# K and V chunks as two interleaved half transfers, and part of one w4 piece in 8-partition transfers

## The chip, the core and the metric

The kernel runs on one core of one Trainium2 chip. The metric is the device time in microseconds (us) of one execution; the median of three executions of the kernel before is 216.05 us (215.88 to 216.5). The core has five instruction streams: TensorE (PE) for matrix products, VectorE (DVE), ScalarE (ACT), GpSimd (POOL) and SyncE (SP). Here SP computes nothing: it issues the transfers from the chip's main memory (HBM) to the on-chip memory (SBUF, 128 partitions), which 16 DMA engines carry out.

## What is computed

One decode step of a transformer block for a batch of four, one token each, width 576. The output is x + attention + MLP, all in bfloat16:

```
xn = layernorm(x)
q  = xn @ wq                          # 32 heads of 128
k, v = the last 2048 positions of the caches, 16 KV heads, each shared by 2 query heads
o  = softmax(q k^T / sqrt(128)) v
A  = o @ wo
h  = gelu(layernorm(xn) @ w1);  x1 = xn + shift(h) @ w2
B  = x1 + gelu(layernorm(x1) @ w3) @ w4     # w3: 576 x 4608, w4: 4608 x 576
out = x + A + B
```

Nearly all of the work is reading: 4 x 16 heads x 2048 positions x 128 values of K and as much of V are 64 blocks of 0.5 MB each, 67 MB together, and the weights are another 21 MB.

## The kernel before

**Chunks.** K and V are each read in 16 chunks (`NC`) of 2 MB. A chunk is one batch row and four KV heads (`NU = 4`). SBUF partition p of a chunk holds head p mod 4 and 64 successive positions, so each partition receives one run of 16 KB from HBM. A ring of four slots (`ring_t`, `NPOS = 4`) holds the chunks. `kv_pairs` (line 226) makes the list of (destination, source) pairs of one chunk; in the kernel before it has one pair, all 128 partitions.

**Transfers.** `add_dma` (line 171) issues one transfer for each pair (line 177) and lets each of them add 16 to one semaphore. SP issues in a fixed order: wq, w2, w1, w3, sixteen K chunks, sixteen V chunks with the first half of wo after the fourth of them, the second half of wo, and then w4 in five pieces. A K chunk waits until the transposes of the chunk four before it are done, a V chunk until its slot is free (lines 232 to 235). SP executes in order, so whatever stands behind a waiting transfer waits too.

**w4.** `W4_ROWS = (18, 9, 6, 2, 1)` cuts the 4608 rows of w4 into pieces of 18, 9, 6, 2 and 1 rows on each of 128 partitions (a row is 576 values, 1152 bytes). The piece numbered 1, the second, is 9 rows: 10,368 bytes on each partition. Each piece has its own semaphore, `("w4", n)`. The first piece waits for early matmuls, the others for nothing; so all five are issued one after another as soon as SP comes to them.

**Compute.** For each K chunk, PE transposes 64 blocks (line 339), DVE and ACT copy them out, and PE multiplies them with the queries (line 353). The softmax follows once for all, and then, for each V chunk, 64 small matmuls (line 420). The attention output is multiplied with wo and the MLP's hidden layer with w4, all adding into the same PSUM tile (line 437); the loop at line 547 takes the w4 pieces in the order in which they were issued, each after a wait for its transfer. The last piece, one row, is followed by two copies (lines 559 and 560) and two small transfers of the output.

**Loops.** The K and V loops on PE are hardware loops. In them a wait for a chunk is a "take": it waits until the semaphore has reached a number and takes that number off again. It is 16 in the kernel before, one transfer's worth. The four ring slots have separate semaphores.

Of the kernel before, what the change touches and what calls it, by code (L numbers as in the profile page):

```python
# [13 lines left out]
NPOS = 4  # L14
ACT_EVAC = (1, 4, 7)
WO_AT = (3.5, 15.5)
IDLE = ((3, -2.7), (7, 0.5), (5, 20.5))
HOPS = (("K", 15), ("V", 2))
W4_ROWS = (18, 9, 6, 2, 1)


# [14 lines left out]
def bass_parallel_sum__sliding_block_cached__mixer_s_mlp__decode_kernel(  # L36
# [3 lines left out]
    _, Hkv, Sk, Dh = A_k_cache.shape  # L40
    Hq = A_wq.shape[1] // Dh
    F = B_w3.shape[1]
    W = min(4096, max(256, Sk // 4))
    assert (B, D, Hkv, Dh, Hq, W, Hq // Hkv, F) == (4, 576, 16, 128, 32, 2048, 2, 4608)
    NU = 4
    NC = B * Hkv // NU
    NI = 128 // NU
    NT = W // NI
    UE = NT * Dh
# [10 lines left out]
    with ExitStack() as ctx:  # L60
        def sb(name, shape, dt):
            return ctx.enter_context(nc.sbuf_tensor(name, shape, dt))
# [4 lines left out]
        ring_t = sb("ring", [128, NPOS * UE], BF16)  # L67
# [89 lines left out]
        def add(engine, emit, waits=(), sig=None, key=0.0, inc=(), loop=None, cond=None):  # L157
            seqc[0] += 1
            prog[engine].append(Op(emit, waits, sig, key, seqc[0], inc, loop, cond))

        def tok(nm):
            if nm not in S:
                S[nm] = sem("t_" + "_".join(str(k) for k in (nm if isinstance(nm, tuple) else (nm,))))
            return nm

        def take(nm, n=1):
            return ("take", tok(nm), n)
# [3 lines left out]
        def add_dma(pairs, skey, waits=(), key=0.0, engine="sp"):  # L171
            tok(skey)
            dma_count[skey] = dma_count.get(skey, 0) + 16 * len(pairs)

            def emit(e):
                for o_, i_ in pairs:
                    e.dma_start(o_, i_).then_inc(S[skey], 16)  # L177
            add(engine, emit, waits, None, key)
            return ("dma", skey, dma_count[skey])
# [11 lines left out]
        def pool_ident(t, tag, pattern, view, key):  # L191
# [19 lines left out]
            waits=["ident_f"], sig="mU", key=-8)  # L211
# [13 lines left out]

        def kv_pairs(cache, c):
            b, gq = CH[c]
            return [(ring_t[:, (c % NPOS) * UE:(c % NPOS + 1) * UE],
                     cache[b, NU * gq:NU * gq + NU, Sk - W:Sk, :].rearrange("g (i t) d -> i g (t d)", t=NT))]

        t_done = lambda c: f"T{NBLK * c + NBLK - 1}"
        for c in range(NC):
            add_dma(kv_pairs(A_k_cache, c), ("k", c % NPOS), [t_done(c - NPOS)] if c >= NPOS else [], c)
# [4 lines left out]
        w4tile, w4cols, ev_w4, W4N = [], [], [], []  # L238
        base = 0
        for n, rc in enumerate(W4_ROWS):  # L240
            v = w4_t[:, len(w4tile) * D:(len(w4tile) + rc) * D]
            ev_w4.append(add_dma([(v, B_w4[base:base + 128 * rc, :].rearrange("(p r) n -> p (r n)", r=rc))], ("w4", n),
                                 ["hT1", "hs1"] if n == 0 else [], KT + 5 + n))
            W4N.append((len(w4tile), len(w4tile) + rc))
            for r in range(rc):
                w4tile.append(v[:, r * D:(r + 1) * D])
                w4cols.append((base + r, base + 128 * rc, rc))
            base += 128 * rc
# [68 lines left out]
        for b in range(B):  # L317
            add("dve", lambda e, b=b: e.tensor_copy(out=qp_out[:, b], in_=qp_in[:, b]), waits=["qTp", "qpad_zero"],
                sig="qT" if b == B - 1 else None, key=-29.4)
# [13 lines left out]
        def pe_T(n):  # L333
            c, k = n // NBLK, n % NBLK

            def f(e):
                ins = None
                for t in range(8):
                    ins = e.transpose(tb[n % 4][:, t, :], slot_t(c)[:, 8 * k + t, :], perm_bf[:])  # L339
                return ins  # L340
            return f

        def evac(n):
            if n % 8 in ACT_EVAC:
                return "act", lambda e: e.activation(out=ktbuf[:, n % 16], in_=tb[n % 4], func=ACTF.Copy)  # L345
            return "dve", lambda e: e.tensor_copy(out=ktbuf[:, n % 16], in_=tb[n % 4])  # L346

        def pe_SC(c):
            def f(e):
                ins = None  # L350
                for q in range(4):
                    for u in range(NU):
                        ins = e.matmul(Sps[32 * u:32 * u + 32, q, :].rearrange("p (t i) -> p t i", t=16),  # L353
                                       lhsT=Qs[:, c % NPOS, 32 * u:32 * u + 32], rhs=ktgrp[:, 4 * (c % 2) + q, :, u, :],
                                       start=False, stop=True, tile_position=(0, 32 * u), skip_group_check=True)
                return ins
            return f
# [3 lines left out]
        for c in range(NC):  # L361
            lp = ("K", c // NPOS)
            for k in range(NBLK):
                w = [take(("k", c % NPOS), 16)] if k == 0 else []
                prev = (k + 4) % 8
                w.append(evtok(prev))
                add("pe", pe_T(NBLK * c + k), waits=w, sig=f"T{NBLK * c + k}", key=NBLK * c + k, loop=lp)
                eng, f = evac(NBLK * c + k)
                add(eng, f, waits=[f"T{NBLK * c + k}"] + ([f"SC{c - 2}"] if c >= 2 else []), inc=[("evA" if eng == "act" else "evD", 1)],
                    key=NBLK * c + k + 0.2)  # L370
            add("pe", pe_SC(c - 1), waits=[take("qs")], sig=f"SC{c - 1}", key=NBLK * c + SC_AFTER + 0.5, loop=lp)
            b, gq = CH[c]
            cc = 4 * b + gq
            P(lambda e, c=c, cc=cc: e.tensor_copy(out=Qs[:, c % NPOS, :], in_=Qpad_t[:, 128 * cc:128 * cc + 128]),  # L374
              waits=["qT", "qs_zero"] + ([f"SC{c - NPOS}"] if c >= NPOS - 1 else []), inc=[("qs", 1)], key=c)
# [6 lines left out]
            waits=["rmax"], sig="negb", key=KS + 0.05)  # L382
        for q in range(4):
            add("act", lambda e, q=q: e.activation(out=P_sb[:, q, :], in_=Sps[:, q, :], func=ACTF.Exp,
                                                   bias=negb[:, 0:1], scale=scale, accum_out=rs4[:, q:q + 1]),
                waits=["negb"], sig=f"exp{q}", key=KS + 0.1 + 0.01 * q)

        for q in range(4):
# [3 lines left out]
                waits=[f"PTx{q}", "permT_bf"] + (["PT0"] if q == 3 else []), sig=f"PTy{q}", key=k0)  # L392
            add("act", lambda e, q=q: e.activation(out=PT_t[:, 512 * q:512 * (q + 1)], in_=ps[:, 4 + q % 3, :], func=ACTF.Copy),
                waits=[f"PTy{q}"], sig=f"PT{q}", key=k0 + 0.16)
# [3 lines left out]
            waits=["rinv", "ident_f"], sig="diag", key=KS + 0.82)  # L398
        add("pe", lambda e: e.matmul(rinvps, lhsT=ones_f[:], rhs=diag[:], start=True, stop=True), waits=["diag", "ones_f", "exp3"],
            sig="rinvp", key=KS + 0.9)  # L400
        add("dve", lambda e: e.tensor_copy(out=rinvB[:].rearrange("p (c u e) -> p c u e", u=NU, e=2),
                                           in_=rinvps.rearrange("p (u c e) -> p c u e", u=NU, e=2)),
            waits=["rinvp"], sig="rinvB", key=KS + 1.5)
# [9 lines left out]
        def pe_PV(c):  # L413
            b, gq = CH[c]
            o_ = OTps[:, 8 * b:8 * b + 8]

            def f(e):
                ins = None
                for t in range(NT):
                    ins = e.matmul(o_, lhsT=slot_t(c)[:, t, :], rhs=PTpad[:, c % 2, t].rearrange("p u e -> p (u e)"),  # L420
                                   start=(t == 0), stop=(t == NT - 1))
                return ins
            return f
        for c in range(NC):
            w = [f"PV{c - 2}"] if c >= 2 else [f"PT{q}" for q in range(4)] + ["mU_bf1"]
            b, gq = CH[c]
            add("dve", dve_pad(c), waits=w, inc=[(tok("pad"), 1)], key=KV + 2 * max(c - 1, 0) + 0.2)
            add("pe", pe_PV(c), waits=[take("pad"), take(("v", c % NPOS), 16)] + ([take("otn")] if b == 0 else []), sig=f"PV{c}",
                key=KV + 2 * c, loop=("V", gq))
            if b == B - 1:  # L430
                hv = lambda t, gq=gq: t[:, 0:128].rearrange("p (b h) -> p b h", b=B)[:, :, 8 * gq:8 * gq + 8]
                add("dve", lambda e, hv=hv: e.tensor_tensor(out=hv(OTn), in0=OTps.rearrange("p (b h) -> p b h", b=B), in1=hv(rinvB), op=ALU.mult),  # L432
                    waits=["rinvB", f"PV{c}"], sig=f"OTn{gq}" if gq == 3 else None, inc=[(tok("otn"), 1)] if gq < 3 else [], key=KV + 2 * c + 0.1)
# [13 lines left out]
        def pe_AO(half):  # L447
# [10 lines left out]
            waits=["OTy"], sig="ORp", key=KT - 2.5)  # L458
# [30 lines left out]
        for h in range(2):  # L489
# [3 lines left out]
                waits=[f"hs{h}", "ln1"], sig="x1" if h else "x1a", key=-29 + 0.6 * h)  # L493
# [4 lines left out]
        for h in range(2):  # L498
            add("act", lambda e, h=h: e.activation(out=h_sb[:, HALF * h:HALF * (h + 1)], in_=HTps[h], func=ACTF.Gelu_apprx_tanh),
                waits=[f"hT{h}", "x1nT"], sig="gelu_h" if h else None, key=-20 + 0.1 * h)  # L500

        segs = []
        for g in range(4):
            for k in range(3):
                first = 9 * g + 3 * k
                t = first
                while t < first + 3:
                    n = next(m for m, (a, z) in enumerate(W4N) if a <= t < z)
                    cnt = min(first + 3, W4N[n][1]) - t
                    segs.append((g, k, t - first, cnt, w4cols[W4N[n][0]][0], W4_ROWS[n], t - W4N[n][0], t == first))  # L510
                    t += cnt
# [18 lines left out]
        for k in range(3):  # L530
            add("act", lambda e, k=k: e.activation(out=h2g[:, 384 * k:384 * (k + 1)], in_=H2ps[k], func=ACTF.Gelu_apprx_tanh), waits=["h2_3"],
                sig="gelu2" if k == 2 else None, key=-0.9 + 0.1 * k)

        def pe_h2T(e):
# [7 lines left out]
            waits=["h2T"], inc=[("evA", 1)], key=-0.3)  # L542
        add("dve", lambda e: e.tensor_copy(out=h2o[:, :, 8, :], in_=H2Tb.rearrange("p (g y) -> p g y", g=4)[..., 0:B]),  # L543
            waits=["h2T"], inc=[("evD", 1)], key=-0.3)
# [51 lines left out]
        def emit_program(eng_name, engine):  # L596
# [6 lines left out]
            while i < len(ops):  # L603
# [12 lines left out]
                with engine.bass.Fori(0, len(passes), engines=OrderedEngineSet([engine.engine]), head_slot={engine.engine: 0}):  # L616
                    inner = nc.cur_bb
                    for k, op in enumerate(passes[0]):
                        emit_op(eng_name, engine, op, waited)
                        if (name, k) in HOPS:  # L620
                            engine.br_eq(hop, 0, on_true=f"hop_{name}", on_false=f"fall_{name}")
# [53 lines left out]
```

## Time and profile before

| | before |
|---|---|
| median of three executions | 216.05 us |
| the profiled execution, its own time | 216.5 us |
| its span, first to last instruction | 214.7 us |
| bytes moved | 88.65 MB |
| PE busy | 147.2 us (69%) |
| DVE busy | 76.2 us (35%) |
| ACT busy | 60.2 us (28%) |
| K transfers, 2048 KB each | 16 |
| V transfers, 2048 KB each | 16 |
| w4 transfers, 2592 / 1296 / 864 / 288 / 144 KB | 1 each |

The profile shows one execution. Its page cuts the span in 40 equal slices of 5.4 us and gives for each the busy share of every engine, of the DMA engines, and the rate of transfer. It lists the queues of the DMA engines (q1 is SP's, "instruction" queues load program code), the chain of work that ended last, and the groups of instructions. "SPq" is SP issuing a transfer. The records behind the page also hold the start, length and size of each packet that a DMA engine moved, and the times at which transfers added to their semaphores; they do not say which of the 16 engines a packet was on.

### The profile page before, as it was taken

The numbers are of one execution on the slowest core, as the hardware profiler recorded it, in microseconds if no ns is written. First come the engines' busy times: TensorE is split into PE (matmuls) and PEld (weight loads), VectorE is DVE, ScalarE is ACT, GpSimd is POOL, SyncE is SP. The second block draws the span as 40 slices with busy tenths as digits, with TensorE's granted clock in tenths as the row PEclk, the third lists the DMA queues.
The fourth block names the chain that finished last, engine by engine and source line by source line (L and its number), as shares of the span: only waits on it lengthen the run. The fifth ranks groups of instructions, "written<-read, shape, count | busy, mean of one in ns | idle before, by whom it ended". The sixth has DMA issues, their size and how long they took to land. (4 is left out here: it accounts for less than half of the span.)

```text
span 214.7 us, 5874 instructions
## 1 busy us (share of the span) xinstructions
PE 147.2 (69%) x2642; PEld 111.2 (52%) x2646; DVE 76.2 (35%) x150; ACT 60.2 (28%) x75; POOL 10.9 (5%) x37
## 2 busy tenths in 40 slices
PE   0158699799999999999997177334444333337984
PEld 0023333777888887788885047234434333335542
DVE  4303700276667767667775751110010010001000
ACT  2001210455666666566666540000000000000000
POOL 8301000000000000000000000000000000000000
PEclk9999889699999999999999755555555555555999
DMA  7999999999999999999999999999999999999992
GB/s 276 409 381 443 436 413 433 437 424 411 412 424 430 433 433 424 427 429 433 421 430 424 427 436 419 427 427 430 424 427 424 430 430 427 427 432 432 417 413 78
DMA packets 6946, 88.65 MB, mean 413 GB/s; under 512 B 780, under 2 KB 1176, under 8 KB 1944
## 3 DMA queue, kind: packets, MB, share of 16 engines
q1 hardware_dynamic: 6920, 88.50, 97.4%
q8 instruction: 8, 0.13, 0.2%
q10 hardware_dynamic: 16, 0.01, 0.0%
q14 instruction: 2, 0.02, 0.0%
HBM read 88.49 MB, written 0.00 MB: 412 GB/s over the span
## 5 line engine op out<-in xcount | busy, mean ns | idle before, releaser
L339 PEld LDWEIGHTS ps<-perm_bf,ring 128*128 128x128 bf16 x1024 | 58.8, 99 | 7.1 <-issue 6.8
L339 PE MATMUL ps<-perm_bf,ring 128*128 128x128 bf16 x1024 | 61.9, 221 | 0.0
L346 DVE COPY kt<-ps 128x1024 bf16<-128x1024 bf16 x80 | 52.3, 688 | 24.2 <-PE ps L339 23.1
L420 PE MATMUL ps<-PTpad,ring 128*128 128x8 bf16 x1024 | 29.7, 168 | 39.9 <-PEq L583 35.9
L345 ACT ACTIVATE kt<-ps 128x1024 bf16<-128x1024 bf16 x48 | 47.7, 1023 | 29.3 <-PE ps L339 29.3
L420 PEld LDWEIGHTS ps<-PTpad,ring 128*128 128x128 bf16 x1024 | 28.7, 104 | 41.1 <-issue 41.0
L560 ACT ACTIVATE out_sb<-ps 4x288 bf16<-4x288 f32 x1 | 0.4, 401 | 86.4 <-PE ps L437 86.4
L353 PE MATMUL ps<-kt,Qs 128*32 128x512 bf16 x272 | 17.8, 382 | 1.4 <-PEq L583 1.4
L409 DVE TENSOR_TENSOR PTpad<-PT,mU_bf 128x512 bf16<-128x512 bf16 x16 | 6.4, 421 | 28.2 <-PE ps L420 28.2
L432 DVE TENSOR_TENSOR OTn<-ps,rinvB 128x32 bf16<-128x32 f32 x4 | 0.8, 192 | 34.5 <-PE ps L420 34.5
L522 PE MATMUL ps<-w,x1nT 128*32 128x384 bf16 (+1 forms) x65 | 11.1, 766 | 0.4 <-DVE x1nT L497 0.4
L353 PEld LDWEIGHTS ps<-kt,Qs 128*32 128x32 bf16 x272 | 5.8, 95 | 6.8 <-issue 1.5
L374 POOL COPY Qs<-Qpad 128x128 bf16<-128x128 bf16 x16 | 4.6, 293 | 89.1 <-PE ps L353 75.9
L300 PE MATMUL ps<-kt,xnT 128*32 128x512 bf16 x32 | 3.6, 631 | 4.6 <-DMA kt<-in_A_wq_dram 4.6
L522 PEld LDWEIGHTS ps<-w,x1nT 128*32 128x32 bf16 x65 | 3.6, 115 | 5.4 <-issue 5.0
L277 PE MATMUL ps<-ident_bf,xn_bf 4*128 4x4 bf16 x8 | 0.6, 170 | 8.0 <-DVE ragsrc L270 8.0
L437 PE MATMUL ps<-w,h2T_sb 128*4 128x288 bf16 x72 | 5.1, 286 | 1.4 <-DMA w<-in_B_w_dram 1.4
L559 DVE CAST out_sb<-ps 4x288 bf16<-4x288 f32 x1 | 0.4, 446 | 14.9 <-PE ps L437 14.9
L437 PE MATMUL ps<-w,ORT 128*4 128x288 bf16 x64 | 5.0, 324 | 0.4 <-DVE ORT L459 0.4
L391 PE MATMUL ps<-kt,permT_bf 128*128 128x512 bf16 x3 | 1.8, 608 | 4.9 <-DVE kt L390 4.8
L437 PEld LDWEIGHTS ps<-w,h2T_sb 128*4 128x4 bf16 x72 | 2.8, 84 | 4.0 <-DMA w<-in_B_w_dram 3.0
L543 DVE COPY h2T_sb<-ps 128x16 bf16<-128x16 bf16 x1 | 0.2, 166 | 13.3 <-PE ps L537 13.3
(99 smaller groups left out, 65.2 us busy)
## 6 DMA issues: line engine op xcount, KB each, us to landing
ring<-in_A_k_cache_dram SPq DMA_DIRECT2D x16, 2048.0 KB, 11.5
ring<-in_A_v_cache_dram SPq DMA_DIRECT2D x16, 2048.0 KB, 16.6
w<-in_B_w_dram SPq DMA_DIRECT2D x2, 2304.0 KB, 23.0
w<-in_A_wo_dram SPq DMA_DIRECT2D x2, 2304.0 KB, 20.3
kt<-in_A_wq_dram SPq DMA_DIRECT2D x1, 4096.0 KB, 12.5
w<-in_B_w_dram SPq DMA_DIRECT2D x1, 2592.0 KB, 28.0
w<-in_B_w_dram SPq DMA_DIRECT2D x3, 576.0 KB, 14.3
w<-in_B_w_dram SPq DMA_DIRECT2D x1, 1296.0 KB, 30.7
```

Source lines behind the costliest of these rows:

```text
L300: ins = e.matmul(Qps[k][32 * g:32 * g + 32, :], lhsT=x_, rhs=w, start=(r == 0), stop=(r == 4), tile_position=(0, 32 * g), skip_group_check ...
L339: ins = e.transpose(tb[n % 4][:, t, :], slot_t(c)[:, 8 * k + t, :], perm_bf[:])
L345: return "act", lambda e: e.activation(out=ktbuf[:, n % 16], in_=tb[n % 4], func=ACTF.Copy)
L346: return "dve", lambda e: e.tensor_copy(out=ktbuf[:, n % 16], in_=tb[n % 4])
L353: ins = e.matmul(Sps[32 * u:32 * u + 32, q, :].rearrange("p (t i) -> p t i", t=16), lhsT=Qs[:, c % NPOS, 32 * u:32 * u + 32], rhs=ktgrp[:, ...
L374: P(lambda e, c=c, cc=cc: e.tensor_copy(out=Qs[:, c % NPOS, :], in_=Qpad_t[:, 128 * cc:128 * cc + 128]), waits=["qT", "qs_zero"] + ([f"SC{ ...
L391: add("pe", lambda e, q=q: e.matmul(ps[:, 4 + q % 3, :], lhsT=permT_bf[:], rhs=PTx[:, q, :], start=True, stop=True), waits=[f"PTx{q}", "pe ...
L409: return lambda e: e.tensor_tensor(out=PTpad[:, c % 2], in0=PTv[:, :, cc, :].unsqueeze(2).to_broadcast([128, NT, NU, 2]), in1=mU_bf[:].uns ...
L420: ins = e.matmul(o_, lhsT=slot_t(c)[:, t, :], rhs=PTpad[:, c % 2, t].rearrange("p u e -> p (u e)"), start=(t == 0), stop=(t == NT - 1))
L432: add("dve", lambda e, hv=hv: e.tensor_tensor(out=hv(OTn), in0=OTps.rearrange("p (b h) -> p b h", b=B), in1=hv(rinvB), op=ALU.mult), waits ...
L437: return e.matmul(ACC[h], lhsT=lhsT, rhs=rhs, start=start, stop=stop, tile_position=(0, 32 * h), skip_group_check=True)
L522: ins = e.matmul(H2ps[k][32 * g:32 * g + 32, 128 * off:128 * (off + cnt)].rearrange("p (c x) -> p c x", c=cnt), lhsT=x_, rhs=w.rearrange(" ...
```

## The change

There are two edits. First, `kv_pairs` gives two pairs for each chunk: the even partitions (`a = 0`, heads 0 and 2 of the four) and the odd ones (`a = 1`, heads 1 and 3), 64 partitions and 1 MB each. The takes of the two loops become 32. The bytes, the size of a run on one partition (16 KB) and the order of the chunks stay.

Second, `LOW8 = 1` names the w4 piece 1. Its partitions 0, 4, 8, ..., then 1, 5, 9, ..., then 2, 6, 10, ... are loaded by three transfers of 32 partitions, and the last quarter, partitions 3, 7, 11, ..., by four transfers of 8 partitions. The description of the change says that only DMA engines 0 to 7 carry those last four. The other pieces stay.

```
+LOW8 = 1
 W4_ROWS = (18, 9, 6, 2, 1)
...
         def kv_pairs(cache, c):
             b, gq = CH[c]
-            return [(ring_t[:, (c % NPOS) * UE:(c % NPOS + 1) * UE],
-                     cache[b, NU * gq:NU * gq + NU, Sk - W:Sk, :].rearrange("g (i t) d -> i g (t d)", t=NT))]
+            dst = lambda a: ring_t[a:128:2, (c % NPOS) * UE:(c % NPOS + 1) * UE]
+            src = cache[b, NU * gq:NU * gq + NU, Sk - W:Sk, :].rearrange("g (i t) d -> i g (t d)", t=NT)
+            return [(dst(a), src[:, a:NU:2, :]) for a in range(2)]
...
             v = w4_t[:, len(w4tile) * D:(len(w4tile) + rc) * D]
-            ev_w4.append(add_dma([(v, B_w4[base:base + 128 * rc, :].rearrange("(p r) n -> p (r n)", r=rc))], ("w4", n),
+            w4_src = B_w4[base:base + 128 * rc, :].rearrange("(p r) n -> p (r n)", r=rc)
+            rows = [slice(0, 128)] if n != LOW8 else [slice(a, 128, 4) for a in range(3)] + [slice(3 + a, 32 + a, 4) for a in range(0, 128, 32)]
+            ev_w4.append(add_dma([(v[a], w4_src[a]) for a in rows], ("w4", n),
                                  ["hT1", "hs1"] if n == 0 else [], KT + 5 + n))
...
-                w = [take(("k", c % NPOS), 16)] if k == 0 else []
+                w = [take(("k", c % NPOS), 32)] if k == 0 else []
...
-            add("pe", pe_PV(c), waits=[take("pad"), take(("v", c % NPOS), 16)] + ([take("otn")] if b == 0 else []), sig=f"PV{c}",
+            add("pe", pe_PV(c), waits=[take("pad"), take(("v", c % NPOS), 32)] + ([take("otn")] if b == 0 else []), sig=f"PV{c}",
```

## The prediction

> **What bounds the kernel now.** I read the DMA rows of the page first, then the chain that ended last, then SP's queue.
>
> ```profile
> span 214.7 us, 5874 instructions
> PE   0158699799999999999997177334444333337984
> DMA  7999999999999999999999999999999999999992
> GB/s 276 409 381 443 436 413 433 437 424 411 412 424 430 433 433 424 427 429 433 421 430 424 427 436 419 427 427 430 424 427 424 430 430 427 427 432 432 417 413 78
> q1 hardware_dynamic: 6920, 88.50, 97.4%
> q8 instruction: 8, 0.13, 0.2%
> ```
>
> The DMA row is 9 from the second slice to the last but one, also where PE falls to 3: the transfers are the bound throughout. SP's queue alone fills 97.4% of the 16 engines. The packet records say what the rate is made of: a 16 KB packet takes 611 ns (26.8 GB/s on one engine, 429 on sixteen; the stretches between 60 and 178 us show 427 to 429). Each engine carries 8 packets per chunk, and chunks land 4.89 us apart, which is 8 x 611 ns. There is no gap between transfers to win.
>
> ```profile
> DMA 15%; PE 1%; SPq 1%; DVE 0%; issue 0%
> DMA w<-in_B_w_dram 15%; SPq L177 1%; PE ps L420 1%; PE ps L437 0%; DVE out_sb L559 0%
> ...
> 178.91 32.92 DMA w<-in_B_w_dram
> 211.84 0.04 issue
> 211.88 0.58 PE ps L437 x6
> 212.46 0.43 DVE out_sb L559
> ```
>
> The chain ends on the w4 pieces: issued by 179.4, landed at 211.84 and later, then 0.58 us of matmul, 0.43 us of copy and the output. So the end is set by the DMA engine that finishes its share last. The semaphore records show how far the sixteen are apart: a transfer adds 16, one per engine, and for the last piece these come at 209.58 (first), eight by 210.72, and the other eight from 211.28 to 212.06. There are two groups. The spread was 0.61 us in the first transfer; the late engines each jump once by about 1.55 us. The eight jumps fall where the eight 16 KB packets of q8, program code, run (29.4, 43.1, 52.6, 120.3, 129.4, 135.9, 159.3 and 209.7 us, each 1.02 to 1.10 us long), each time on an engine not hit before. So half of the engines have lost one code load each and never make it up, because nothing balances the load.
>
> ```profile
> 45.99 0.54 SPq L177 DMA_DIRECT2D ring<-in_A_k_cache_dram  x1
> 177.49 2.33 SPq L177 DMA_DIRECT2D w<-in_B_w_dram  x5
> ring<-in_A_k_cache_dram SPq DMA_DIRECT2D x16, 2048.0 KB, 11.5
> ring<-in_A_v_cache_dram SPq DMA_DIRECT2D x16, 2048.0 KB, 16.6
> SPq L177 <- PE ps L339: 100.9, 16, 32.7
> SPq L177 <- PE ps L420: 52.7, 12, 11.7
> ```
>
> SP is idle most of the time, waiting for ring slots, and a K chunk is issued 11.5 us before it lands, of which its own packets take 4.9.
>
> **Part 1, two transfers for a chunk.** Removed: 32 issues of 0.535 us. Added: 64. If a half costs the same, SP is busy 17 us longer, inside 153 us of waits. The second half follows the first by about 0.58 us and then queues behind it; for the tightest chunk (issued at 45.99, when the three before it still have packets until 49.2) there are 3.2 us in hand. Had the cover been gone, each such late issue would stop the engines for up to 0.58 us. At the start SP stands in the first K issue for 5.84 us because the queue is full; eight half issues instead of four end some 2 us later than 13.8, and K is first read at 29. The tail: six more w4 issues of 0.43 us and the second half of the last V chunk end SP's issuing at about 183 instead of 179.8; the last piece's packets start at 208.8. All that is free. A take of 32 waits for the later half, whose last packet is the same last packet as before; PE and, behind it, SP's next issue see no change.
>
> What is not free is on the engines: each transfer ends with a 4-byte packet on each engine that adds to the semaphore, 9 ns in the records. 32 more are 0.29 us per engine. Lower bound 0 (8 x 611 ns is already 4.89, so it may be hidden), upper bound 0.29 us plus 0.05 for piece 1; I take 0.3.
>
> [...]
>
> An unknown remains: which partitions an engine writes when a transfer names every second one. No row shows a transfer of 64 strided partitions. If two engines then share a way into SBUF and meet there, a packet could take up to twice 611 ns: 256 K and V packets per engine x 611 ns = 156 us. If they don't meet, 0. All the rows near it (packets of 4 KB to 32 KB over 128 partitions, all at 26 to 27 GB/s) are at one engine's own speed, so I take 0 and keep the upper end as a rival. A gain is excluded here: a packet cannot use more than its engine, and the engines are full.
>
> **Part 2, piece 1.** One transfer becomes seven. A row of one partition is a packet of 10,368 bytes, 389 ns. Before, each engine has 8 of them, 3.11 us. After, by the description, engines 0 to 7 have 2 + 2 + 2 from the three transfers of 32 partitions and 4 from those of 8: ten, 3.89 us. Engines 8 to 15 have six, 2.33 us. So one half gets 0.78 us later, the other 0.78 us earlier, and stays so through pieces 2 to 4, which queue behind. PE's wait for piece 1 (112 counts) is passed at the landing of the later group; it is followed by waits for pieces 2 to 4 that land later still.
>
> So everything hangs on whether engines 0 to 7 are the late group or the early one. The trace does not number the engines. What it has: the first transfer's packets start one after another from 1.91 to 2.54 us, about 42 ns apart, as if handed to one engine after another; and following the packets of each engine, most of the late ones are among the first eight starters (two or three could not be followed surely). If the engines are served in order of number, the late ones are engines 0 to 7, and the change loads the wrong half.
>
> **Sum.** Late group: + 0.78 + 0.3 = + 1.1 us on the last landing, and all behind it shifts by as much. The profiled execution took 216.5 us (span 214.7 and 1.8 around it), 0.45 above the median; on the median, 216.05 + 1.1 = 217.15 us.
>
> **Rivals.**
>
> (a) *Engines 0 to 7 are the early group.* For it: the early half has 1.3 us of slack at the end (210.72 against 212.06). Late group 212.06 - 0.78; early group 210.72 + 0.78 = 211.50, which then is last: - 0.56 + 0.3 = - 0.26 us, 215.8 us. Not slower. At the best the last of the early ones (its second-last landed at 210.47) is in the other half and the semaphore packets are hidden: - 0.78 us, 215.3 us. It decides as soon as the eight engines hit by code loads are mostly 8 to 15; against it is the order of the first packets.
>
> (b) *Engines meet on their way into SBUF* in the strided transfers. [...] From nothing to + 156 us; with one packet in fifty hit, + 3 us.
>
> (c) *The 8-partition transfers are not confined* to eight engines, so piece 1 is spread evenly: only the 0.3 us remain, 216.35 us.
>
> **How the numbers follow.** A measurement of this kernel can tell about 0.3%, 0.65 us, from no change. Late group loaded: 0.42, of which 0.36 slower and 0.06 same. (a): 0.32, of which 0.22 same and 0.10 faster. (b): 0.12, slower. (c): 0.10, of which 0.08 same and 0.02 slower. 0.04 is left for a gain that no row shows, faster. Sum: faster 0.14, same 0.36, slower 0.50. The range leaves out most of (b), 0.1, and that last 0.04: from 215.1 (the best of (a), and a little for the spread of the executions) to 218.5 (the 1.1 us, the 0.6 us that three executions are apart, and a little of (b)).
>
> **What would show it.** Chunks should land 4.89 to 4.90 us apart, and GB/s stay at 427 between 60 and 178 us; if it falls, (b). Piece 1 should have ten packets of 10,368 bytes on eight engines and six on the others; if eight each, (c). At the last piece the two groups should be 0.78 + 0.78 us further apart than 1.4 us, so about 3 us; if they have closed up to under 0.5 us, (a). I would be wrong above all if the order of the first packets is not the order of the engines' numbers.

## The result and the profile after

The changed kernel takes 218.13 us (median of six executions, 217.94 to 218.82) against 216.04 us (215.88 to 216.5, six). The ratio is 1.0098, 95% interval 1.0081 to 1.0115: about 2.1 us slower. Forecast was 217.15 us, so the direction was right and the amount about half. The experiments below show that most of the amount came from something that the forecast's sum left out.

These are lines of the page of the kernel after: the span, the DMA rows in 40 slices, SP's queue, and the chain that ended last.

```profile
span 216.3 us, 5912 instructions
DMA  8999999999999999999999999999999999999992
GB/s 286 394 390 448 419 430 433 421 420 427 433 424 433 433 418 427 432 421 436 430 424 424 427 427 428 430 427 421 430 430 421 436 424 423 430 430 433 412 283 76
q1 hardware_dynamic: 7496, 88.50, 97.6%
DMA 14%; SPq 3%; PE 2%; issue 0%; DVE 0%
```

The engines are as busy as before, to the last slice but one. But in that slice, 205.5 to 210.9 us, they move 283 GB/s. Up to there the two kernels run alike: the second half of wo lands from 197.09 us on, before from 197.19. So the K and V half transfers, which fill 160 us of the span, cost nothing, and all of the loss lies behind 205 us.

The same place in stretches of 2 us (the columns after the engines' busy times are the granted TensorE clock, the DMA engines' busy share and GB/s), first before, then after:

```profile
204.00:206.00 2.00, 1.26 (x12) 0.53 (x12) 0.00 (x0) 0.00 (x0) 0.00 (x0) 1.00 0.99 418
206.00:208.00 2.00, 2.00 (x33) 1.30 (x30) 0.00 (x0) 0.00 (x0) 0.00 (x0) 1.00 0.98 415
208.00:210.00 2.00, 2.00 (x21) 1.00 (x21) 0.00 (x0) 0.00 (x0) 0.00 (x0) 1.00 0.92 368
```

```profile
204.00:206.00 2.00, 1.85 (x18) 0.84 (x18) 0.00 (x0) 0.00 (x0) 0.00 (x0) 1.00 0.96 404
206.00:208.00 2.00, 2.00 (x30) 1.22 (x27) 0.00 (x0) 0.00 (x0) 0.00 (x0) 1.00 1.01 270
208.00:210.00 2.00, 0.88 (x5) 0.20 (x2) 0.00 (x0) 0.00 (x0) 0.00 (x0) 1.00 1.05 249
210.00:212.00 2.00, 1.16 (x18) 0.71 (x18) 0.00 (x0) 0.00 (x0) 0.00 (x0) 1.00 0.75 279
```

Busy and slow at once: a busy share of 1.01 at 270 GB/s says that packets take longer, not that engines wait. The packet records confirm it. A row of piece 1 (10,368 bytes) took 389 to 398 ns before, all 128 of them. After, 31 took over 1.2 times that, up to 776 ns, and 86 of the 128 packets of piece 2 (6,912 bytes, 262 ns before) went up to 536 ns. Four microseconds at about 260 in place of 427 GB/s is 1.6 us of all sixteen engines.

The end of the chain, after, and two rows of the timeline, which stand behind it:

```profile
183.30 29.30 DMA w<-in_B_w_dram
212.60 0.04 issue
212.64 1.39 PE ps L441 x18
214.03 0.43 DVE out_sb L563
```

```profile
213.70 0.08 PEld L441 LDWEIGHTS ps<-w,h2T_sb 128*4 128x4 bf16 x2 [0.23 <-DMA w<-in_B_w_dram]
214.02 0.45 DVE L563 CAST out_sb<-ps 4x288 bf16<-4x288 f32 x1 [16.70 <-PE ps L441]
```

The chain names the landing of piece 2, at 212.60, and 18 matmuls behind it. But among these PE waits once more for a transfer: its last two weight loads start at 213.70, 0.04 us after the last engine has landed the last piece (213.66). Before, the last piece landed at 212.06, and in both kernels the copy starts 0.4 us behind that landing. So the last landing is 1.60 us later, and everything behind it is later by as much: the spans are 214.7 and 216.3 us. The medians are 2.1 us apart, because the profiled execution before (216.5 us) is the slowest of its six and the one after (218.0) the second fastest. That 18 matmuls now run in one group is no loss: in the run with four transfers of 32 partitions, below, the same group takes 1.40 us, and that kernel is as fast as the one before.

### The profile page after: what moved, and what is told of

The parts are those of the page before. It is cut to its first block, busy times and chain, and to the rows that moved or that the text cites. A ratio compares the mean times of both kernels' runs of the same rounds, so it can differ in the third digit from the quotient of the medians.

```text
span 216.3 us, 5912 instructions
## 1 busy us (share of the span) xinstructions
PE 145.3 (67%) x2642; PEld 108.8 (50%) x2646; DVE 76.2 (35%) x150; ACT 61.1 (28%) x75; POOL 11.0 (5%) x37
## 5 line engine op out<-in xcount | busy, mean ns | idle before, releaser
L343 PEld LDWEIGHTS ps<-perm_bf,ring 128*128 128x128 bf16 x1024 | 57.5, 98 | 9.1 <-issue 9.0
L349 ACT ACTIVATE kt<-ps 128x1024 bf16<-128x1024 bf16 x48 | 48.6, 1024 | 29.3 <-PE ps L343 28.3
L526 PE MATMUL ps<-w,x1nT 128*32 128x384 bf16 (+2 forms) x65 | 11.3, 765 | 0.6 <-DMA w<-in_B_w_dram 0.6
L441 PE MATMUL ps<-w,ORT 128*4 128x288 bf16 x64 | 5.6, 350 | 0.4 <-DVE ORT L463 0.4
```

The lines of the kernel that those rows point to most:

```text
L441: return e.matmul(ACC[h], lhsT=lhsT, rhs=rhs, start=start, stop=stop, tile_position=(0, 32 * h), skip_group_check=True)
L526: ins = e.matmul(H2ps[k][32 * g:32 * g + 32, 128 * off:128 * (off + cnt)].rearrange("p (c x) -> p c x", c=cnt), lhsT=x_, rhs=w.rearrange(" ...
```

## Experiments

The theory formed from these lines: engines 0 to 7, which by the description carry the 8-partition transfers, write into partitions that other engines are writing at the same time, and they hinder each other. Rivals were the number of transfers, the strided half transfers, and the load alone.

**One part at a time.** First the half transfers alone. This is the kernel after with a number that no piece of w4 has, so that none is cut:

```
-LOW8 = 1
+LOW8 = -1
```

> The K and V chunks as two half transfers, w4 piece 1 as one transfer again. Theory (all of the loss is in piece 1): the same as the kernel before within 0.3 us, chunks 4.89 us apart, second wo half starting to land at 197.1 us as in both kernels. Rival (the 32 added transfers cost their semaphore packets, 9 ns each, or more): 0.3 us slower or more, 216.35 us and up.

Measured: 215.99 us, ratio 1.0001 (0.9991 to 1.0012). Its stretches:

```profile
60.00:110.00 50.00, 49.97 (x851) 41.42 (x848) 34.57 (x54) 31.09 (x32) 2.64 (x9) 1.00 1.01 429
110.00:178.00 68.00, 30.71 (x869) 26.79 (x870) 15.40 (x33) 10.20 (x17) 0.00 (x0) 0.57 1.01 427
```

They show the rates of the kernel before, and the second half of wo starts to land at 197.19 us, as there. The 512 added semaphore packets (1293 of 4 bytes in place of 781) are in the trace, and they don't show in the time: the upper end of the interval is 0.26 us, and the lower bound, 0, fits.

Then the cut of piece 1 alone, in the kernel before:

```
...
+            rows = [slice(0, 128)] if n != 1 else [slice(a, 128, 4) for a in range(3)] + [slice(3 + a, 32 + a, 4) for a in range(0, 128, 32)]
...
```

> Piece 1 in seven transfers, the chunks whole. Theory: all of the loss, + 1.6 to + 2.1 us, with rows of 10,368 bytes in the four 8-partition transfers taking up to 776 ns in place of 389, and the packets of piece 2 about 440 in place of 262. Rival (the two parts need each other: half transfers leave the engines in another order): under half of the loss, below 217.1 us.

Measured: 218.3 us, ratio 1.0104 (1.0089 to 1.0119). All of the loss is here: 31 rows slow, up to 813 ns, and 98 packets of piece 2. The two parts don't need each other.

**The number of transfers and their stride.**

```
...
+            rows = [slice(0, 128)] if n != 1 else [slice(a, 128, 4) for a in range(4)]
...
```

> Piece 1 in four transfers of 32 partitions (every fourth), none of 8; the chunks whole. Theory (the 8-partition transfers are the trouble, not the number of transfers or the stride): same as before within 0.3 us, all rows at 389 ns. Rival (strided small transfers slow the engines): 0.5 us or more slower, rows above 389 ns.

Measured: 216.06 us, ratio 0.9999 (0.999 to 1.0008), no row above 396 ns. Neither several transfers nor a stride of four partitions cost anything. Every row goes from the same place in HBM to the same partition as in the run with seven transfers; only the grouping differs, and with it how many engines carry a transfer: the 80 landings of piece 1 in the change are three times sixteen and four times eight. What is left is the 8-partition transfers.

**Where they write.** The next kernel puts extra loads of w4 rows (`p_src`, the rows of piece 1) between the V chunks, into columns of `kt` that nobody reads any more (`p_dst`). The output is unchanged, and the total time is longer by the extra loads.

```
...
+        PROBES = ((4, [slice(3, 32, 4), slice(35, 64, 4)]), (7, [slice(67, 96, 4), slice(99, 128, 4)]),
+                  (10, [slice(0, 64, 8), slice(1, 64, 8)]), (13, [slice(2, 128, 4)]))
+        for c, sl in PROBES:
+            ev_p = add_dma([(p_dst[a, j, :], p_src[a]) for a in sl for j in range(2)], ("probe", c), [], KS + c + 0.2)
...
```

> The kernel before with extra loads of w4 rows into a dead part of kt in the V phase, which change nothing in the output: after V chunk 4 four transfers of 8 partitions into partitions 3 to 63 (every fourth); after chunk 7 four into 67 to 127 (every fourth); after chunk 10 four into partitions 0, 8, .. 56 and 1, 9, .. 57; after chunk 13 two of 32 partitions (every fourth). Theory A (engines 0 to 7 meet engines 8 to 15 on the way into the upper partitions): rows at 389 ns after chunk 4, up to 776 after chunk 7, and 16 KB packets beside the latter up to twice 611. Theory B (any transfer on eight engines slows all): all three sets slow, the set of 32 not. Theory C (an engine has eight neighbouring partitions of its own): slow after chunks 4 and 7, not after 10. Whichever holds, the engines 0 to 7 get 1.56 us later at each of the first three sets; if these are the late ones, the spread of a chunk's landings (1.9 to 2.2 us) grows by that, and if they are the early ones it shrinks first.

Measured: 230.44 us, in one execution. The stretches of its trace (the first holds the set behind chunk 4, the second the one behind chunk 7, the fourth the one behind chunk 10, the last the transfers of 32 partitions):

```profile
132.00:152.00 20.00, 7.88 (x273) 7.64 (x274) 2.06 (x6) 0.00 (x0) 0.00 (x0) 0.50 1.01 427
154.00:159.00 5.00, 0.53 (x20) 0.56 (x21) 0.00 (x0) 0.00 (x0) 0.00 (x0) 0.50 0.98 216
161.00:171.00 10.00, 1.85 (x64) 1.79 (x64) 0.64 (x2) 0.00 (x0) 0.00 (x0) 0.50 1.01 426
174.00:179.00 5.00, 0.00 (x0) 0.00 (x0) 0.00 (x0) 0.00 (x0) 0.00 (x0) 0.50 1.04 193
183.00:200.00 17.00, 5.54 (x192) 5.37 (x192) 1.71 (x5) 0.00 (x0) 0.00 (x0) 0.50 1.01 428
```

And the packets (median, ns; beside a set are the packets of V that started between its first row's start and its last row's end):

```
set                       10,368-byte rows   16 KB packets of V beside them
3 .. 63, every 4th        389                611
67 .. 127, every 4th      772                1131
0 .. 56 and 1 .. 57, /8   831                1145
2 .. 126, 32 at a time    389                612
```

This parts the theories. A transfer on eight engines is not slow in itself: the lower set runs at 389 ns a row and leaves the V packets at 611. The upper set, by the description on the same engines, with rows of the same size from the same piece of w4, halves the rate of everything, 216 GB/s in place of 427. The set with a stride of 8 does so too (831 ns, 193 GB/s), though it stays in the lower half; so "an engine owns eight neighbouring partitions" (theory C) is out. Which partitions an engine writes is in no record, and no run shows why the place decides; shown is that it does.

The jam reaches engines that, by the description, carry no row of the set. Of the 16 KB packets that started between 174 and 178 us, beside the set with a stride of 8, none took less than 1246 ns, on any engine. How they come to be slowed was not separated further, and the trace doesn't number engines.

The probe run also shows which engines are late. Behind the lower set, eight engines have their next landing 1.56 us later, and eight don't. The landings of the V chunk ahead of it lay at 0 to 2.48 us after the first; the shifted ones were those at 0, 0.01, 0.18, 0.25, 0.98, 1.23, 1.62 and 2.21, the unshifted those at 0, 0.34, 0.50, 0.60, 1.66, 1.75, 1.89 and 2.48. If the shifted ones are 0 to 7, as the description has it, late engines are in both halves: in this execution two of the six then beyond 1.6 us are among 0 to 7, four among 8 to 15.

**Load against place, at the end of the kernel.** Two extra transfers of 8 partitions behind piece 1, again into unused columns, in one kernel the lower ones, in another the upper ones:

```
...
+        ev_p = add_dma([(p_dst[a, :], p_src[a]) for a in [slice(3, 32, 4), slice(35, 64, 4)]], "extra", [], KT + 6.5)
...
```

```
...
+        ev_p = add_dma([(p_dst[a, :], p_src[a]) for a in [slice(67, 96, 4), slice(99, 128, 4)]], "extra", [], KT + 6.5)
...
```

The two differ in the destination and in which rows of piece 1 they read. The source is not what counts: with four transfers of 32 partitions all rows of piece 1 had taken 389 to 396 ns. Each puts two rows of 389 ns, 0.78 us, on the eight engines that by the description are 0 to 7. The expectations from here on speak of the partitions of an engine, of foreign ones and of ways in: that is the theory they test, not a reading of a record. Shown is place and time, 389 ns for a row of the lower set, 772 for one of the upper.

> The kernel before, and behind w4 piece 1 two more transfers of 8 partitions, 3 to 63 every fourth, into a dead part of kt (10,368 bytes for each partition, nothing in the output). [...] If some of the late engines are among 0 to 7: + 0.5 to + 0.8 us, 216.55 to 216.85 us, no packet above its usual time. If all the late ones are among 8 to 15: under 0.1 us.

> The same with partitions 67 to 127, every fourth: the same load on the same engines, only the place that it is written to differs. Theory (engines 0 to 7 writing into the partitions of 8 to 15 put all writes on half of the ways in): 0.8 to 1.7 us over the run with the lower partitions, 217.4 to 218.5 us, with rows at up to 776 ns and packets of 6,912 bytes at 430 or more. Rival (only the load counts): the same time as the run with the lower partitions.

Measured: lower 216.44 us, ratio 1.0018 (1.0007 to 1.0029); upper 218.04 us, ratio 1.0095 (1.0081 to 1.0109). The lower, then the upper one between 206 and 210 us:

```profile
206.00:208.00 2.00, 2.00 (x33) 1.25 (x28) 0.00 (x0) 0.00 (x0) 0.00 (x0) 1.00 0.97 410
208.00:210.00 2.00, 2.00 (x23) 1.00 (x21) 0.00 (x0) 0.00 (x0) 0.00 (x0) 1.00 0.95 382
```

```profile
206.00:208.00 2.00, 2.00 (x33) 1.24 (x28) 0.00 (x0) 0.00 (x0) 0.00 (x0) 1.00 1.04 271
208.00:210.00 2.00, 1.04 (x5) 0.29 (x3) 0.00 (x0) 0.00 (x0) 0.00 (x0) 1.00 1.00 246
```

The load alone, 0.78 us on engines 0 to 7, costs 0.47 us (0.15 to 0.63). From the landings of the probe run an estimate is 0.51: the latest of engines 0 to 7 stood at 2.21 and comes to 2.99, the last of all stood at 2.48. The place costs 1.60 us more; the last landings of the two profiles, 212.18 and 213.80 us, are 1.62 apart. The change has the same two upper transfers, two lower ones, and takes two rows off engines 8 to 15; it lost 2.1 us.

The profiled execution with the upper set took 219.1 us, the median is 218.04. It lost another microsecond behind the last landing:

```profile
212.77 2.37 PE ps L441 x18
```

The granted clock was 0.70 from 212 to 214 us and 0.50 from 214 to 216, and the 18 matmuls took 2.37 us; at a clock of 1.00, in the change, they took 1.39.

**The amount.** First the cut on the shorter piece 2; after it, on piece 1, one transfer of 16 partitions in place of the two upper ones of 8:

```
...
+            rows = [slice(0, 128)] if n != 2 else [slice(a, 128, 4) for a in range(3)] + [slice(3 + a, 32 + a, 4) for a in range(0, 128, 32)]
...
```

> The cut of the change on w4 piece 2 (6 rows in place of 9), the chunks whole. Theory: the loss goes with the bytes, two thirds of the 2.25 us that it cost on piece 1, so + 1.5 us, 217.55 us. Rival (a fixed cost of seven transfers close to the end): 2 us or more.

Measured: 217.09 us, ratio 1.0054 (1.0039 to 1.007), so 1.1 us, below both expectations. Only 25 packets of piece 2 were slow. The stretch 208 to 210 us moved 303 GB/s, but 206 to 208 us still 412: the jam begins later. That it finds fewer engines with work left is the likely reason, but was not tested.

```
...
+            rows = [slice(0, 128)] if n != 1 else [slice(a, 128, 4) for a in range(3)] + [slice(3, 32, 4), slice(35, 64, 4), slice(67, 128, 4)]
...
```

> Piece 1 in three transfers of 32 partitions, two of 8 for the lower last quarter and one of 16 for the upper (67 to 127 every fourth). If a transfer of 16 goes to the 16 engines by place in the list, engines 0 to 7 write 8 rows into foreign partitions, half of what the change has: about half of its collisions, + 0.8 to + 1.4 us, slow rows and packets as there but for half as long. If it is dealt by partition to the engines that own them: no slow packet, under 0.3 us.

Measured: 216.88 us, ratio 1.0039 (1.0024 to 1.0055), 0.9 us. 23 rows of piece 1 were slow, up to 673 ns, where the change had 31 up to 776. A transfer of 16 partitions is not free of the jam either, which speaks for dealing by place in the list; the dealing itself is in no record.

**Dealing by place, at full size.**

```
...
+            rows = [slice(0, 128)] if n != 1 else [slice(0, 64), slice(64, 128)]
...
```

> w4 piece 1 in two transfers of 64 neighbouring partitions, 0 to 63 and 64 to 127, the chunks whole. If a transfer is dealt to the sixteen engines by place in its list, half of its rows are foreign to the engine that carries them and all go into one half of the partitions: the 3.1 us of piece 1 at half speed, about + 3 us, 219 us, rows near 776 ns. If rows always go to the engine that owns their partition, no collision, 216.0 us.

Measured: 221.14 us, ratio 1.0239 (1.0217 to 1.0261). Ahead of piece 1 and through it:

```profile
196.00:203.00 7.00, 6.62 (x67) 3.54 (x66) 0.58 (x2) 0.00 (x0) 0.00 (x0) 0.64 1.02 430
203.00:212.00 9.00, 5.88 (x57) 2.59 (x52) 0.00 (x0) 0.00 (x0) 0.00 (x0) 1.00 0.99 235
```

122 of the 128 rows are slow, and the rate is 235 GB/s for nine microseconds. Just ahead of the piece it is 430. The cost, 5 us, is more than the 3.1 expected, for two reasons. Packets of the pieces ahead and behind are slow as well: the last landing is at 215.68 us, 3.62 later than in the profile before. And the last 18 matmuls took 2.37 us, at a granted clock of 0.66 from 214 to 216 us and 0.50 from 216 to 218. Halves of every second partition, in the first run, had cost nothing (1.0001); two of neighbouring ones cost 2.4% of this kernel for one piece of 1.3 MB.

The last run has two extra transfers of 8 partitions once more, now with a stride of 8 in the lower half (0, 8, .. 56 and 1, 9, .. 57); by the description engines 0 to 7 alone carry them, and 8 to 15 get no row:

```
...
+        ev_p = add_dma([(p_dst[a, :], p_src[a]) for a in [slice(0, 64, 8), slice(1, 64, 8)]], "extra", [], KT + 6.5)
...
```

> [...] If only engines that meet are slow: engines 8 to 15 keep 262 ns for the packets of piece 2, and the loss lies between that of the lower (0.4 us) and the upper ones (2.1 us). If a jam spreads to all: no less than 2.1 us, 218.1 us or more, with the packets of piece 2 slow on all sixteen engines.

Measured: 218.85 us, ratio 1.0113 (1.0086 to 1.0141). The interval overlaps that of the upper set (1.0081 to 1.0109), so it costs about as much, although only the lower half is written. In the profiled execution, 220.42 us, the last 18 matmuls took 2.37 us here too, at a granted clock of 0.50. The 31 packets of piece 2 that started between 207.2 and 208.9 us took 400 ns or more, all of them, against 262, and the rows of 10,368 bytes that started between 207.3 and 208.4 took 700 ns or more. The records show 16 packets under way at that time, so all the engines were slow, as with the probe of the same kind.

No version of this change that beats the kernel before came out of it. Relieving engines 8 to 15 through 0 to 7 meant transfers of 8 or 16 partitions above 63 too, and there a quarter of a piece cost more in the jam (2.1 us in the change) than balance can bring: before, the last engine is only about 1.2 us behind the mean of all sixteen.

## Why the prediction was half right

The direction was right, and most of the reading of the profile: the DMA engines bound the kernel; the end is the last engine's; SP's 38 further issues and the longer waits cost nothing. SP ended its w4 issues at 184.8, where 183 was expected, and the last piece's packets begin after 209. The first K issue held SP for 5.92 us, against 5.84 before, and ended in both when about as many packets of SP's queue were done (105 and 103); that a full queue held it fits this, but how much the queue takes is in no record.

*Part 1* was put at + 0.3 us. It measured 0.0 (1.0001, 0.9991 to 1.0012, so 0.26 us at the most), and in the change chunks still land 4.89 us apart. The lower bound of that term was nearer: the semaphore packets don't show beside the data packets, as the 4.89 us for 8 x 611 ns had already suggested. The 32 further transfers of SP's cost 0.26 us at the most, all together. The rival that engines meet in the strided transfers was wrong where I looked for it: with the halves alone the rate stayed at 429 and 427 GB/s. Its factor of two, and with it the 156 us and the 3 us, was an assumption, and no run shows that engines share a way into SBUF; what the runs show in its place is that a row of piece 1 takes 389 ns or up to 831, according to where its transfer writes.

*Part 2* is the step that failed. It counted the rows of an engine and priced each at 389 ns, "ten, 3.89 us". The count fits the records: piece 1 has 80 landings, three times sixteen and four times eight, and the lower probe set delayed eight engines by 1.56 us, four rows. The price was wrong: the rows of the upper 8-partition transfers, and everything beside them, took about twice as long (772 against 389 ns and 1131 against 611 in the probe run), which is 1.6 us, measured by the two extra loads, lower and upper. I had weighed this mechanism for the half transfers, with its price of up to twice the packet, and not for the transfers that the description itself says are carried by eight engines into all 128 partitions. There the question was plainest: no row of the kernel before shows eight engines alone carrying transfers that reach all over the 128 partitions.

*The late half.* I took the late engines to be mostly 0 to 7, from the order of the first packets. The probe run, with the description's numbering, shows them in both halves, more of them in 8 to 15. By that count rival (a) was nearer; by the price the main reading was, since two late engines among 0 to 7 are enough to lose: the term of + 0.78 us measured + 0.47 with the load added alone (1.0018).

*The sign at the last piece.* The prediction expected two groups of engines about 3 us apart if the late group was loaded. The sixteen landings do spread over 2.90 us, 210.76 to 213.66, against 2.48 before. That looks like a confirmation and is none, for there are no two groups of eight: three engines land by 211.05 and thirteen from 211.99 on, which fits slow packets on most of them.

*The tail.* That a late last landing shifts "all behind it by as much" held: the last landing came 1.60 us later, and the span is 1.6 us longer.

*Luck.* Two terms were 0.3 us too large each, and 1.6 us was left out; the errors offset each other in part, and the sum looked better than its parts. The direction owes something to luck as well. The load without the jam would have cost an estimated 0.5 us, which is less than the 0.65 us that the prediction called no change; what made the loss clear was the slow packets, which the sum did not have.

## What to carry to other kernels

When a DMA-bound kernel is to be cut into other transfers, ask for each how many engines carry it and which partitions it writes. A cut into every second (1.0001) or every fourth partition (0.9999) over all 128 cost nothing here; transfers of 8 partitions into every fourth above 63, or into every eighth below, brought the rate of all sixteen down from about 427 GB/s to between 193 and 271, in the probes, the change and the run with the upper set. A DMA share of 1.0 beside a falling GB/s row is how it looks (1.01 at 270 GB/s in the change): engines busy with slow packets. Before balancing engines, measure which are late with a small extra load on a known group, and price the move with a second one at the place where it will write.

## What I had not expected

Two transfers of 8 partitions, 0.17 MB in all, cost 1.6 us more for being written to partitions 67 to 127 instead of 3 to 63 (218.04 against 216.44 us). And a jam among the lower partitions alone left no packet at its usual time: 1246 ns at least for 16 KB in place of 611, between 174 and 178 us. Code loads are another: eight of 16 KB, each on another engine, cost that engine about 1.55 us, although a data packet of the size takes 0.61. And in the profiles of three runs the last 18 matmuls took 2.37 us in place of 1.39, at a granted clock that fell to 0.50.
